# Three chained layers on one core: copies moved between engines, half of the split jobs moved to a later stage, a memset between record scatters

## The chip, the cores and the metric

One NeuronCore of a Trainium2 chip runs one program. The metric is the device time of one execution in microseconds (us), the median of three runs. The engines are named PE (TensorE matmul, with PEld for its weight loads), DVE (VectorE), ACT (ScalarE), POOL (GpSimd) and SP (SyncE, which here does little but issue DMAs). A `q` behind a name is that engine's queue of instructions or transfers.

## The reference

The output of each function is the input of the next:

```
def attn(x, h):                      # x (4, 5696, 128), h (5696, 128)
    L = 2 * S
    y = irfft(rfft(x, n=L, axis=1) * rfft(h, n=L, axis=0), n=L, axis=1)[:, :S]

def moe(x, phi, w1, w2):             # x (22784, 128), phi (128, 32): 8 experts, 4 slots each
    logits = x @ phi
    d = softmax(logits, axis=0);  slot_input = d.T @ x
    slot_out[e] = relu(slot_input[e] @ w1[e]) @ w2[e]
    return softmax(logits, axis=1) @ slot_out

def moe2(x, modality_id, w_gate, modality_bias, w1, w2):   # 8 experts, 128 -> 1024 -> 128
    logits = x @ w_gate + modality_bias[modality_id]
    e_idx = argmax(logits); gate_w = softmax(logits)[e_idx]
    out[t] = gate_w[t] * (relu(x[t] @ w1[e]) @ w2[e]),  e = e_idx[t]
```

## The kernel before, in words

**Convolution** (`conv_spectra`, to about 337 us of the span). The long convolution is a product of spectra, and the transforms are matrix products with constant tables. The sequences h and then four batches of x pass one after the other: 16 blocks `psa` (L122) whose result four copies in `columns` spread into A, two on ACT (L127) and two on DVE (L133), and then products `psx` (L188), multiplications on DVE and POOL, and transposes. `load` fetches the next sequence over SP's queue. Beside this runs a side task, the **split jobs** (`w2split_jobs`): the 32 pieces of `moe2_w2` are fetched (`wa`, 128 KB each, L312), cast on ACT (L317), subtracted on DVE (L318) and stored as a high and a low part into `s_wsc` (L320). Seven jobs run in the blocks of each batch of x, one more at i = 18, the rest at the end.

**Slot logits** (`slot_logits`). 32 tiles `psi` (L400), three buffers of PSUM, copied out by ACT (L403) and DVE (L405) by turns. SP loads for this and the next step in this order: two big `yl` (L373), four `Bt` (L381), four ring buffers (L352), then eight `c_iv` (L381). Then `psb` (L421) and the maxima.

**Slot inputs** (`slot_inputs`). `less` (L534) subtracts the maximum, three small pieces on DVE and seven large ones on POOL, and ACT takes the exponential (L538). `columns` makes 16 blocks `psw` with the same four copies; where its `swap` holds, the second copy of the first half goes to DVE (L131) in place of ACT. Then 23 rounds of `px` (L568), a copy on DVE (L569) and `psS` (L575), with the ring of loads beside them; the slot experts follow, whose weights are loaded last.

**Routing and routed experts.** The gate picks an expert for each token, and positions `posi` in a list sorted by expert. `scatter` (L1036) writes 178 columns of 128 records (136 bytes each) into `s_rec` with indirect DMAs on POOL, one instruction for each column. Up to 90 tiles of 256 tokens then run: `load_rec`, `ph` (L1126), ReLU on ACT and a subtraction on DVE (L1128, L1129), `acc` (L1139 to L1141), a transpose, and two indirect scatters into the output on POOL (`store`, L1164). A tile can't start before the first columns are scattered that can hold its records: tile 0 needs 18, tiles 5 to 8 need 34, 14 to 23 need 64, 24 to 39 need 96, 40 to 55 need 128, and from tile 56 on all 178. The order on POOL is written out beforehand by `share`: 64 records, 3 output scatters, 78 records, then records and output scatters in turn, and at the end only output scatters; with the last record 46 output scatters (23 tiles) stand ahead of it. `YBUF = 31` buffers hold finished tiles that wait for their scatter.

```
n = NG - len(pending)
late = max(0, len(outs) - 2 * YBUF + 6)
new = max(0, GB[chunk_of(k + 3) + 1] - n, min(ready[0] - n, m - late))
scatter(new)
store(max(late, m - new), k - 2)
```

Of the kernel before, what the change touches and what calls it, by code (L numbers as in the profile page):

```python
# [12 lines left out]
F32 = mybir.dt.float32  # L13
# [74 lines left out]
def dma89(eng, out, in_):  # L88
    eng.dma_start(out[0:80], in_[0:80])
    eng.dma_start(out[80:N1], in_[80:N1])  # L90
# [6 lines left out]
def keep_warm(nc, pp, t, n, **k):  # L97

    ps = pp.tile([128, 128], F32, name="warm", **k)
    for _ in range(n):  # L100
        nc.tensor.matmul(ps, t, t, start=True, stop=True)
# [14 lines left out]
def columns(nc, tc, pp, xs, fw1, put, swap=False, **k):  # L116


    ps = pp.tile([128, 4, 256], F32, **k)
    pv = ps[:, :, :4 * NPAIR].rearrange("p i (r k e) -> p r i k e", r=2, e=2)  # L120
    for i, x in enumerate(xs):
        nc.tensor.matmul(ps[:, i, :4 * NPAIR], x, fw1, start=True, stop=True)  # L122
    for j in range(2):
        for r in range(2):
            o, v = put(r, j), pv[64 * j:64 * j + 64, r]
            if j == 0 and not (swap and r):
                i = nc.scalar.copy(o, v)  # L127
                tc.declare_no_dep(i.ins, group="half1", reason="other lanes of PSUM, other columns of the result")
                tc.add_to_no_dep_group("half0", i.ins)
            elif j == 0:  # L130
                nc.vector.tensor_copy(o, v)  # L131
            else:
                i = nc.vector.tensor_copy(o, v)  # L133
                tc.declare_no_dep(i.ins, group="half0", reason="other lanes of PSUM, other columns of the result")
                tc.add_to_no_dep_group("half1", i.ins)


def conv_spectra(nc, tc, I, R, P, jobs, xr, ahead):

    G, ident, phi, fw1 = P["G"], P["ident"], P["phi"], P["fw1"]  # L140
    with tc.tile_pool(name="p1", bufs=1) as sp, tc.tile_pool(name="p1p", bufs=2, space=PS) as pp:
# [14 lines left out]
            else:  # L156
                nc.gpsimd.tensor_copy(o, v)  # L157

        def load(q, c):

            if q < len(seqs):
                kind, b = seqs[q]
                src = (I["x"][b] if kind == "x" else I["h"]).rearrange("(p s) d -> p s d", s=N2)
                dma89(nc.sync, xt[:, 16 * c:16 * c + 16], src[:, 16 * c:16 * c + 16])

        def st1(c):

# [2 lines left out]
                    lambda r, j: A[64 * r:64 * r + 64, :, 64 * j + d:64 * j + d + 4].rearrange("p k d e -> p d k e"),  # L170
                    name="psa", tag="psa", bufs=2)

        for c in range(4):
            load(0, c)
        keep_warm(nc, pp, P["ones"], NWARM, tag="psa", bufs=2)

        pl = pp.tile([128, 4, 128], F32, name="psl", tag="psl", bufs=1)
# [93 lines left out]
        for q in range(len(seqs)):  # L271
            z = Seq(q)
            if q == 0:
                for c in range(NXS):
                    spread(c)
            for c in range(16):
                st1(c)
                if c + NXS < 16:
                    spread(c + NXS)
                if q > 0 and jobs and c % 2 and c < 14:  # L280
                    jobs.pop(0)(sp)
                if q == 0 and c < 6:
                    P["loadG"](c)
            for i in range(NB):
                for _ in range(2 if i == 0 else 1):
                    if tail:
                        tail.pop(0)()
                z.step(i)
                if q > 0 and i == 18 and jobs:
                    jobs.pop(0)(sp)  # L290
                if i % 4 == 0 and i < 16:
                    load(q + 1, i // 4)
                if q + 1 < len(seqs) and i % 2 and i >= NB - 2 * NXS:
                    spread((i - NB) // 2 + NXS, nc.scalar)
                if q == B and i % 2 == 0 and 2 <= i < 18:
                    ahead(i // 2 - 1)
            tail = z.tail()
        for t in tail:
            t()
        while jobs:  # L300
            jobs.pop(0)(sp)
def w2split_jobs(nc, I, R):

    got = {}
    n = 4 * NE

    def job(k):
        def run(sp):
            if k < n:
                e, h = divmod(k, 4)  # L310
                a = got[k] = sp.tile([128, 2, 128], F32, name="wa", tag="wa", bufs=2)
                nc.sync.dma_start(a, I["moe2_w2"][e].rearrange("(c p) d -> p c d", p=128)[:, 2 * h:2 * h + 2])  # L312
            if k >= 1:
                e, h = divmod(k - 1, 4)
                a = got.pop(k - 1)
                w = sp.tile([128, 2, 2, 128], F32R, name="ws", tag="ws", bufs=2)
                nc.scalar.copy(w[:, 0], a)  # L317
                nc.vector.tensor_tensor(w[:, 1], a, w[:, 0].bitcast(F32), op=ALU.subtract)  # L318
                o = R["wsc"][e].rearrange("p (r f) -> p r f", r=2)[:, :, 256 * h:256 * h + 256]
                nc.sync.dma_start(o, w.rearrange("p r c d -> p r (c d)").bitcast(F32))  # L320
        return run
    return [job(k) for k in range(n + 1)]
# [35 lines left out]
        return s.rearrange("p (b k d) -> p b k d", b=B, k=YB)[:, b, k % YB, :]  # L358


def slot_logits(nc, tc, I, R, P, a2, xr, yr, Lf):

    ident, ones, iv1 = P["ident"], P["ones"], P["iv1"]
    L = Lf.rearrange("p (j s) -> p j s", s=N2)
# [2 lines left out]
    with tc.tile_pool(name="p2", bufs=1, reuse_waits="tile") as sp, tc.tile_pool(name="p2p", bufs=3, space=PS, reuse_waits="tile") as pp:  # L367
# [7 lines left out]
        def load_B(c):  # L375
            if c < NBT or c >= N2 // BC - NBT:
                t = sp.tile([128, BC, 2, N1], F32, name="Bt", tag="Bt", bufs=NBT)
            else:
                w = 2 * BC * N1
                t = xr[:, w * (c - NBT):w * (c - NBT) + w].rearrange("p (x r s) -> p x r s", x=BC, r=2)  # L380
            nc.sync.dma_start(t, I["c_iv2"][:, BC * c:BC * c + BC])  # L381
            Bt[c] = t
# [9 lines left out]
        pst = [pp.tile([128, 4, 128], F32, name=f"psi{i}", tag=f"a{i}", bufs=1) for i in range(3)]  # L392
        for t in pst:
            nc.vector.memset(t[64:], 0.0)
        for b in range(B):
            yl = yls[b].rearrange("p (k s) -> p k s", s=NS)
            for s in range(0, NS, 4):
                ps = pst[(b * NS + s) // 4 % 3]
                for j in range(4):
                    nc.tensor.matmul(ps[:N1, j], yl[:, :, s + j], iv1, start=True, stop=True)  # L400
                o = A2[:96, :, b * NS + s:b * NS + s + 4].rearrange("p x j -> p j x")
                if s % 8 == 0:
                    nc.scalar.copy(o, ps[:96])  # L403
                else:
                    nc.vector.tensor_copy(o, ps[:96])  # L405
            if b == 1:
                for c in range(NBT, N2 // BC - NBT):
                    load_B(c)
        SC = 8
        mx = sp.tile([N1, N2 // 4, NS], F32, name="mx")  # L410
        m1 = sp.tile([N1, NS], F32, name="m1")
# [101 lines left out]
def slot_inputs(nc, tc, I, R, P, a2, yr, L, cm, c, prefetch, cT):  # L513

    G, fw1 = P["G"], P["fw1"]
    with tc.tile_pool(name="p3p", bufs=2, space=PS, reuse_waits="tile") as pp:
# [8 lines left out]
        jobs = row_softmax_jobs(nc, R, c, scratch(NG))  # L525
        Ssb, den = scratch(128), scratch(NS)
        fill = token_bias(nc, I, scratch(2 * NG), scratch(2 * NE))
        assert used[0] <= 14 * F
        JC = 16

# [10 lines left out]
        less(0, 4, nc.vector)  # L541
        less(4, 8, nc.vector)
        less(8, JC, nc.vector)
        for j in range(JC, 128, JC):
            less(j, j + JC, nc.gpsimd)
        weights(0, 4)
# [1 line left out]
        weights(8, JC)  # L548
        for j in range(0, 128, 8):
            columns(nc, tc, pp, [L[:, j + i:j + i + 2].rearrange("p j s -> p (j s)") for i in (0, 2, 4, 6)], fw1,  # L550
                    lambda r, i: AW[64 * r:64 * r + 64, :, j + i:j + i + 7:2].rearrange("p k j e -> p j k e"), j % 24 == 8,
                    name="psw", tag="a", bufs=2)
            if j + JC < 128:
                weights(j + JC, j + JC + 8)
            if j % JC == JC - 8:
                yr.load()
# [7 lines left out]
        def X(i):  # L564
            n = nk4(i)
            ps = pp.tile([128, 4, 128], F32, name="px3", tag="x", bufs=2)
            for m in range(n):
                nc.tensor.matmul(ps[:, m], G[:, 4 * i + m, :], AW[:, 2 * i + m // 2, :, m % 2], start=True, stop=True)  # L568
            nc.vector.tensor_copy(fw[i % 2][:, :n], ps[:, :n])  # L569

        def dot(i):
            for m in range(nk4(i)):
# [435 lines left out]
def routed_experts(nc, tc, R, P, out, ro, tabs):  # L1008

    ident, rec, posi = P["ident"], ro.rec, ro.posi  # L1010
    with tc.tile_pool(name="p6", bufs=1, reuse_waits="tile") as sp, tc.tile_pool(name="p6p", bufs=1, space=PS, reuse_waits="tile") as pp:
# [20 lines left out]
        def scatter(n):  # L1032
            for _ in range(n):
                c, g = pending.pop(0)
                need(0, g + 1)
                i = nc.gpsimd.indirect_dma_start(R["rec"], bass.IndirectOffsetOnAxis(ap=posi[:, g:g + 1], axis=0), rec[:, g, :], None,  # L1036
                                                 bounds_check=SPARE * TM - 1, oob_is_err=False)
                for q in range(NC):
                    tc.declare_no_dep(i.ins, group=f"rec{q}", reason="positions of tokens are distinct")
                tc.declare_no_dep(i.ins, group="recl", reason="a tile is loaded after its last token was scattered")  # L1040
                tc.declare_no_dep(i.ins, group="pad", reason="rows after the last token")
                tc.add_to_no_dep_group(f"rec{c}", i.ins)
# [203 lines left out]
def build(nc, tc, I, O, dbg=None):  # L1246
# [14 lines left out]
    with tc.tile_pool(name="const", bufs=1) as cp:  # L1261
# [35 lines left out]
            n = min(N1, k + 23)  # L1297
            nc.sync.dma_start(x[:, k:n], R["ylt"][b, :, k:n])
        with tc.manual_schedule():
            conv_spectra(nc, tc, I, R, P, w2split_jobs(nc, I, R), xr,  # L1300
                         ahead)

        pac, pa = pool("pa")
# [19 lines left out]
            for h in range(4):  # L1323
                nc.sync.dma_start(mw[:, 2 * h:2 * h + 2], I["moe2_w1"][2 * h:2 * h + 2].rearrange("e p f -> p e f"))
        with tc.manual_schedule():
            cm = slot_logits(nc, tc, I, R, P, a2, xr, yr, Lf)
        cqc, cq = pool("cq", side="right")
        c = cq.tile([128, NG, NS], F32, name="c")
        g2 = G.rearrange("p k x -> p (k x)")
# [143 lines left out]
```

## Time and profile before

| | |
|---|---|
| median of 3 runs | 1235.42 us (1233.53 to 1237.55) |
| the profiled execution, its own time | 1235.99 us |
| its span, first to last instruction | 1234.2 us |
| busy: PE, DVE, ACT, POOL | 931.4, 651.2, 594.4, 581.0 us |
| instructions | 23513 |
| mean granted TensorE clock | 0.878 |

Busy time counts an engine's instructions that compute or, on POOL, prepare a DMA. The page's slices cut the span into 40 equal parts of 30.9 us; a digit is the busy share in tenths. The chain is followed back from the last instruction, at each step to what released it. "Another core or an unknown queue" is a stretch for which the trace shows no releaser, and "issue" one in which the engine waited for nothing that the profile shows.

### The profile page before, as it was taken

The page shows a single profiled execution, that of the slowest core. Times are in us where ns is not written, and L with a number is a line of the kernel's source. Part 1 is how long each engine was busy: PE and PEld are TensorE (multiplying, and loading weights), DVE is VectorE, ACT ScalarE, POOL GpSimd, SP SyncE. Part 2 cuts the span into 40 slices and gives each one's busy share as a digit, 9 for nine tenths or more (in the row PEclk, how much of TensorE's full clock was granted, in tenths as well). Part 3 has the DMA queues.
Part 4 walks back from the last instruction along what each step waited for, and adds up shares of the span by engine and source line. Part 5 has one row for each costly group of instructions (what it writes and reads, how often), then busy time and mean ns, then how long its engine had stood idle before and what let it go on. Part 6 is the DMA issues. An engine that isn't in the chain of part 4 may idle for free.

```text
span 1234.2 us, 23513 instructions
## 1 busy us (share of the span) xinstructions
PE 931.4 (75%) x7670; PEld 845.8 (69%) x7670; DVE 651.2 (53%) x1225; ACT 594.4 (48%) x1338; POOL 581.0 (47%) x677
## 2 busy tenths in 40 slices
PE   7989999999999789933189231810119999999996
PEld 7988888888799777613189231810119999999996
DVE  2577767777637885432068121600016666666663
ACT  2574747565544542210068021600017777777774
POOL 2127566565830433157701755277554444444443
PEclk8999999999999999966589665965559999999999
DMA  9437585766783889833110000011001111111112
GB/s 290 106 92 221 155 233 177 217 193 188 251 313 106 292 288 399 262 88 114 27 47 11 15 13 12 13 30 32 28 29 42 38 38 40 37 40 38 40 39 77
DMA packets 101901, 144.20 MB, mean 117 GB/s; under 512 B 26044, under 2 KB 80764, under 8 KB 99228
## 3 DMA queue, kind: packets, MB, share of 16 engines
q1 hardware_dynamic: 90056, 126.82, 32.9%
q0 software_dynamic: 11456, 14.79, 4.0%
q8 instruction: 64, 1.05, 0.4%
q10 hardware_dynamic: 264, 1.05, 0.2%
q14 instruction: 61, 0.50, 0.1%
HBM read 220.23 MB, written 57.77 MB: 225 GB/s over the span
## 4 chain that ended last, share of the span: by engine, by line
PE 62%; another core or an unknown queue 17%; DVE 9%; issue 5%; ACT 4%; DMA 2%; POOL 0%; SPq 0%; ACTq 0%; POOLq 0%; DVEq 0%
PE psx L188 9%; PE ph L1126 8%; PE acc L1141 7%; PE acc L1140 7%; PE acc L1139 7%; PE psa L122 6%; PE psi L400 3%; PE psy L94 3%; PE pso L94 3%; DVE A L133 3%; PE psl L226 2%; PE psb L421 2%; PE psS L575 1%; PE px L568 1%
## 5 line engine op out<-in xcount | busy, mean ns | idle before, releaser
L1129 DVE SCALAR_TENSOR_TENSOR hl<-ph,hh 128x512 fp32r<-128x512 f32 x360 | 247.9, 691 | 256.4 <-issue 134.5
L1164 POOL DMA_INDIRECT out<-y,rt x180 | 174.9, 972 | 218.4 <-ACT y L1153 173.6
L1128 ACT ACTIVATE hh<-ph 128x512 fp32r<-128x512 f32 x360 | 216.2, 602 | 107.3 <-PE ph L1126 41.0
L1126 PE MATMUL ph<-x,wm 128*128 128x256 f32 x720 | 164.6, 312 | 103.8 <-issue 65.2
L1036 POOL DMA_INDIRECT s_rec<-rec,posi x178 | 173.4, 974 | 134.9 <-issue 52.9
L1140 PE MATMUL acc<-hl,wo 128*128 128x256 f32 x720 | 208.5, 290 | 3.7 <-issue 3.7
L1141 PE MATMUL acc<-hh,wo 128*128 128x256 f32 x720 | 208.3, 289 | 3.5 <-issue 3.5
L1139 PE MATMUL acc<-hh,wo 128*128 128x256 f32 x720 | 209.0, 290 | 0.3 <-issue 0.3
L1126 PEld LDWEIGHTS ph<-x,wm 128*128 128x128 f32 x720 | 115.0, 199 | 107.4 <-issue 66.4
L1141 PEld LDWEIGHTS acc<-hh,wo 128*128 128x128 f32 x720 | 142.9, 198 | 3.8 <-issue 3.8
L1140 PEld LDWEIGHTS acc<-hl,wo 128*128 128x128 f32 x720 | 143.1, 199 | 2.7 <-issue 2.5
L1139 PEld LDWEIGHTS acc<-hh,wo 128*128 128x128 f32 x720 | 142.9, 198 | 0.0
L188 PE MATMUL psx<-G,A 128*128 128x128 f32 x890 | 124.5, 287 | 2.5 <-DVE A L133 1.3
L188 PEld LDWEIGHTS psx<-G,A 128*128 128x128 f32 x890 | 111.9, 196 | 19.8 <-DVE Y L199 13.2
L122 PE MATMUL psa<-fw,xs 128*128 128x180 f32 x640 | 111.0, 328 | 13.0 <-POOL xs L157 6.8
L122 PEld LDWEIGHTS psa<-fw,xs 128*128 128x128 f32 x640 | 100.7, 200 | 23.5 <-POOL xs L157 14.4
L133 DVE COPY A<-psa 64x360 f32<-64x360 f32 x160 | 88.2, 551 | 37.3 <-PE psa L122 33.5
L127 ACT COPY A<-psa 64x360 f32<-64x360 f32 x160 | 83.6, 522 | 42.2 <-PE psa L122 39.0
L201 POOL TENSOR_TENSOR Y<-Y,V 128x256 f32<-128x256 f32 (+1 forms) x92 | 65.4, 711 | 63.8 <-DVE V L200 57.8
L94 PE MATMUL pso<-ident,yT 128*128 128x128 f32 x180 | 39.9, 305 | 71.1 <-ACT yT L1145 50.6
L212 ACT COPY yt<-psy 128x512 f32<-128x512 f32 (+1 forms) x92 | 52.6, 572 | 79.4 <-PE psy L94 50.2
L157 POOL COPY xs<-xr 89x512 f32<-89x512 f32 x68 | 45.7, 673 | 94.6 <-PE psa L122 74.1
(200 smaller groups left out, 1414.2 us busy)
## 6 DMA issues: line engine op xcount, KB each, us to landing
wo<-s_wsc SPq DMA_DIRECT2D x90, 1024.0 KB
wm<-s_mwsc SPq DMA_DIRECT2D x180, 256.0 KB
s_yt<-yt SPq DMA_DIRECT2D x88, 256.0 KB
xr<-x SPq DMA_DIRECT2D x16, 640.0 KB
xr<-s_yt SPq DMA_DIRECT2D x18, 512.0 KB
s_wsc<-ws SPq DMA_DIRECT2D x32, 256.0 KB
L<-s_yt SPq DMA_DIRECT2D x16, 512.0 KB
s_ylt<-ylt SPq DMA_DIRECT2D x20, 256.0 KB
```

The source lines that it names most:

```text
L94: nc.tensor.transpose(out, in_, ident)
L122: nc.tensor.matmul(ps[:, i, :4 * NPAIR], x, fw1, start=True, stop=True)
L133: i = nc.vector.tensor_copy(o, v)
L188: nc.tensor.matmul(ps[:, m, :], A[:, 2 * i + m // 2, :, m % 2], G[:, 4 * i + m, :], start=True, stop=True)
L1036: i = nc.gpsimd.indirect_dma_start(R["rec"], bass.IndirectOffsetOnAxis(ap=posi[:, g:g + 1], axis=0), rec[:, g, :], None, bounds_check=SPAR ...
L1126: nc.tensor.matmul(ps[:, TM * j:TM * j + TM], wm[k % 3][:, 128 * f:128 * f + 128], x[k], start=True, stop=True)
L1128: nc.scalar.activation(o, ps, AF.Relu)
L1129: nc.vector.scalar_tensor_tensor(hl[:, 2 * q:2 * q + 2].rearrange("p j t -> p (j t)"), ps, 0.0, o.bitcast(F32), op0=ALU.max, op1=ALU.subtract)
L1139: nc.tensor.matmul(acc[k], wh, hh[:, f], start=(f == 0), stop=False)
L1140: nc.tensor.matmul(acc[k], wh, hl[:, f], start=False, stop=False)
L1141: nc.tensor.matmul(acc[k], wl, hh[:, f], start=False, stop=(f == 7))
L1164: i = nc.gpsimd.indirect_dma_start(out, bass.IndirectOffsetOnAxis(ap=r[:, j, NS + 1:RW].bitcast(I32), axis=0), y[:, j, :], None, bounds_ch ...
```

## The change

- h is loaded half over SP's and half over ACT's queue.
- `columns` makes its four copies in the order ACT, DVE, DVE, and last the one that `swap` gives to DVE or leaves to ACT; `swap` holds for 8 of the 16 `psw` blocks, not 5.
- In the convolution the split jobs run at every fourth block, and 16 of 32 are left for `psi`, where one runs at every second tile, with its buffers in the free end of Lf.
- A one-column copy on POOL (`pause`) waits for the last of DVE's three `less` pieces before POOL starts its own.
- The copies of `px` go to ACT for i < 13.
- A memset of 128x64 on POOL stands ahead of each of the 178 record scatters.

```diff
-    for j in range(2):
-        for r in range(2):
+    for j, r in ((0, 0), (1, 0), (1, 1), (0, 1)):
...
+            load(0, c + 2, nc.scalar)
...
-                if q > 0 and jobs and c % 2 and c < 14:
+                if q > 0 and c % 4 == 3 and c < 14:
                     jobs.pop(0)(sp)
...
-        while jobs:
-            jobs.pop(0)(sp)
+        jobs[0](sp, load=False)
...
+        free = 2 * YLW
+        def split(name, k):
+            if name == "wa":
+                return Lf[:, free + 256 * (k % 3):free + 256 * (k % 3) + 256].rearrange("p (c d) -> p c d", c=2)
+            w = Lf[:, free + 768 + 512 * (k % 3):free + 768 + 512 * (k % 3) + 512]
+            return w.rearrange("p (r c d) -> p r c d", r=2, c=2).bitcast(F32R)
...
                     nc.vector.tensor_copy(o, ps[:96])
+                if jobs and s % 8 == 0:
+                    jobs.pop(0)(split)
...
+        nc.gpsimd.tensor_copy(pause, L[:N1, JC - 1, :1])
         for j in range(JC, 128, JC):
             less(j, j + JC, nc.gpsimd)
...
-                    lambda r, i: AW[64 * r:64 * r + 64, :, j + i:j + i + 7:2].rearrange("p k j e -> p j k e"), j % 24 == 8,
+                    lambda r, i: AW[64 * r:64 * r + 64, :, j + i:j + i + 7:2].rearrange("p k j e -> p j k e"), j % 16 == 8,
...
-            nc.vector.tensor_copy(fw[i % 2][:, :n], ps[:, :n])
+            if i < 13:
+                nc.scalar.copy(fw[i % 2][:, :n], ps[:, :n])
+            else:
+                nc.vector.tensor_copy(fw[i % 2][:, :n], ps[:, :n])
...
                 need(0, g + 1)
+                nc.gpsimd.memset(P["iv1"][:, :64], 0.0)
                 i = nc.gpsimd.indirect_dma_start(R["rec"], bass.IndirectOffsetOnAxis(ap=posi[:, g:g + 1], axis=0), rec[:, g, :], None,
```

POOL at the start of the routing, before (the routed lists begin with the identity's cast, L1371; `s_rec<-rec,posi` is a record scatter, `out<-y,rt` an output scatter):

```order
L1371 CAST identr<-ident 128x128
L1036 DMA s_rec<-rec,posi 184576x34 x18
L806 IOTA rec 128x42
L1036 DMA s_rec<-rec,posi 184576x34 x46
L1164 DMA out<-y,rt 22784x128 x3
L1036 DMA s_rec<-rec,posi 184576x34 x78
```

The same place of POOL after the change (`iv_77` is iv1, no longer read by then):

```order
L1389 CAST identr<-ident 128x128
L1052 MEMSET iv_77 128x64
L1053 DMA s_rec<-rec,posi 184576x34
L1052 MEMSET iv_77 128x64
L1053 DMA s_rec<-rec,posi 184576x34
```

A memset stands ahead of each scatter, so no two record scatters stand next to each other; the output scatters have none.

SP at the loads for `psi` after the change (L372 and L380 are L373 and L381 of before, L351 is L352; `L<-moe_w` is a load of `wa`, `s_wsc<-L` a store of a split):

```order
L372 DMA L<-s_ylt 128x2848 x2
L380 DMA Bt<-c_iv 128x712 x4
L351 DMA xr<-s_yt 128x1024 x2
L351 DMA ring<-s_yt 128x1024 x2
L311 DMA L<-moe_w 128x2x128 x2
L319 DMA s_wsc<-L 256x1x256
L311 DMA L<-moe_w 128x2x128
```

DVE in the first tiles of `psi` after the change; ACT has a cast (L316) in the same way after each of its copies but the first:

```order
L393 MEMSET psi_3456 64x512
L412 COPY A_3425<-psi_3455 96x4x128
L317 TENSOR_TENSOR L<-L 128x256
L412 COPY A_3425<-psi_3454 96x4x128
L317 TENSOR_TENSOR L<-L 128x256
L412 COPY A_3425<-psi_3456 96x4x128
```

In the list of before the copies stand one after the other; now a step of a split job, which waits for a load that SP issues behind ten others, stands between the first and the second copy of DVE. The eight `c_iv` loads that followed the ring loads now stand behind seven of these stores.

## Rows read from the trace of the kernel before

**Rows 1.** The page: busy tenths in 40 slices, and the chain by engine.

```profile
PE   7989999999999789933189231810119999999996
POOL 2127566565830433157701755277554444444443
...
PE 62%; another core or an unknown queue 17%; DVE 9%; issue 5%; ACT 4%; DMA 2%; POOL 0%; SPq 0%; ACTq 0%; POOLq 0%; DVEq 0%
```

**Rows 2.** The chain, 530 to 930 us, two long pieces: start, us, what.

```profile
533.42 19.59 another core or an unknown queue
...
576.30 44.74 another core or an unknown queue
```

**Rows 3.** Stretches: from:to, us, busy us (instructions) by engine, clock, DMA share, GB/s.

```profile
core 0: us, PE busy (x) PEld busy (x) DVE busy (x) ACT busy (x) POOL busy (x), PEclk, DMA share, GB/s
583.00:621.00 38.00, 5.58 (x16) 4.03 (x15) 0.00 (x0) 0.00 (x0) 24.29 (x25) 0.50 0.13 29
799.00:863.00 64.00, 7.17 (x36) 6.58 (x36) 2.37 (x4) 3.36 (x8) 48.63 (x51) 0.58 0.11 31
863.00:883.00 20.00, 0.70 (x3) 0.70 (x4) 0.98 (x2) 1.17 (x3) 9.73 (x11) 0.50 0.07 23
920.00:1226.00 306.00, 298.64 (x2395) 285.49 (x2394) 202.46 (x331) 232.58 (x599) 131.39 (x136) 0.99 0.15 43
```

**Rows 4.** POOL in order of time: start, us, line, idle before and its releaser.

```profile
528.69 0.97 POOL L1036 DMA_INDIRECT s_rec<-rec,posi  x1 [0.30 <-issue]
529.97 0.97 POOL L1036 DMA_INDIRECT s_rec<-rec,posi  x1 [0.30 <-issue]
...
555.28 0.21 POOL L806 IOTA rec<- 128x42 int32 x1 [5.19 <-DVE xr L730]
556.07 1.14 POOL L1036 DMA_INDIRECT s_rec<-rec,posi  x1 [0.58 <-issue]
557.52 0.97 POOL L1036 DMA_INDIRECT s_rec<-rec,posi  x1 [0.30 <-issue]
```

**Rows 5.** Line 1036 alone: count, shortest/median/longest ns, first and last start.

```profile
L1036 POOL DMA_INDIRECT s_rec<-rec,posi x178: 969/972/1169, 527.2 to 919.4; - x178
```

**Rows 6.** PE inside and behind the record burst of 556 to 615 us.

```profile
589.49 0.37 PE L101 MATMUL warm<-ones 128*128 128x128 f32 x1 [2.45 <-issue]
...
623.90 2.07 PE L1126 MATMUL ph<-x,wm 128*128 128x256 f32 x8 [0.46 <-ACT x L1117]
```

**Rows 7.** A memset of nearly this size on POOL.

```profile
504.90 0.16 POOL L1367 MEMSET pad<- 128x68 f32 x1 [27.46 <-PE e L637]
```

**Rows 8.** SP's DMA issues for psi, in order of time.

```profile
338.78 2.34 SPq L373 DMA_DIRECT2D L<-s_ylt  x2
...
350.37 10.38 SPq L381 DMA_DIRECT2D xr<-c_iv  x8
```

**Rows 9.** The same loads: count, KB each.

```profile
xr<-c_iv SPq DMA_DIRECT2D x8, 356.0 KB
```

**Rows 10.** Stretches of psi and px, columns as in the third group.

```profile
337.00:378.00 41.00, 40.93 (x257) 40.63 (x257) 16.54 (x18) 16.89 (x18) 13.03 (x4) 0.96 0.63 241
356.00:364.00 8.00, 8.00 (x53) 8.00 (x53) 3.59 (x4) 3.08 (x3) 0.00 (x0) 1.00 1.03 400
364.00:380.00 16.00, 14.63 (x96) 14.47 (x95) 6.42 (x7) 6.16 (x6) 0.00 (x0) 1.00 0.03 10
446.00:502.00 56.00, 52.53 (x937) 44.24 (x935) 35.60 (x68) 13.22 (x22) 22.95 (x21) 1.00 0.99 353
```

**Rows 11.** Waits of 412 to 446 us (psw): total us, times, longest.

```profile
DVE A L131 <- ACT A L127: 5.7, 5, 1.6
...
ACT L L538 <- DVE L L534: 5.5, 3, 2.1
```

**Rows 12.** Waits of 446 to 502 us (px, psS).

```profile
PEld psS L575 <- DVE A L569: 4.7, 7, 0.8
```

**Rows 13.** The chain of 495 to 525 us, its longest piece.

```profile
507.00 9.07 DMA A<-moe_w
```

**Rows 14.** Waits of 134 to 157 us (the psa blocks of one batch).

```profile
PE psa L122 <- DVE A L133: 1.2, 3, 0.4
```

**Rows 15.** Busy tenths of the DMA engines, 0 to 20 us.

```profile
DMA  0003955999998999999999999999899998699899
```

More of the change, by code (lines that the diff above doesn't have):

```diff
@@ L122, in columns @@
         nc.tensor.matmul(ps[:, i, :4 * NPAIR], x, fw1, start=True, stop=True)
-    for j in range(2):
-        for r in range(2):
[L125 to L135, printed above, removed]
+    for j, r in ((0, 0), (1, 0), (1, 1), (0, 1)):
+        o, v = put(r, j), pv[64 * j:64 * j + 64, r]
+        if j == 0 and not (swap and r):
+            i = nc.scalar.copy(o, v)
+            tc.declare_no_dep(i.ins, group="half1", reason="other lanes of PSUM, other columns of the result")
+            tc.add_to_no_dep_group("half0", i.ins)
+        elif j == 0:
+            nc.vector.tensor_copy(o, v)
+        else:
+            i = nc.vector.tensor_copy(o, v)
+            tc.declare_no_dep(i.ins, group="half0", reason="other lanes of PSUM, other columns of the result")
+            tc.add_to_no_dep_group("half1", i.ins)
 def conv_spectra(nc, tc, I, R, P, jobs, xr, ahead):
@@ L157, in spread, with load @@
                 nc.gpsimd.tensor_copy(o, v)
-        def load(q, c):
+        def load(q, c, eng=nc.sync):
             if q < len(seqs):
@@ L163, in load @@
                 src = (I["x"][b] if kind == "x" else I["h"]).rearrange("(p s) d -> p s d", s=N2)
-                dma89(nc.sync, xt[:, 16 * c:16 * c + 16], src[:, 16 * c:16 * c + 16])
+                dma89(eng, xt[:, 16 * c:16 * c + 16], src[:, 16 * c:16 * c + 16])
         def st1(c):
@@ L171, in st1 @@
                     name="psa", tag="psa", bufs=2)
-        for c in range(4):
+        for c in range(2):
             load(0, c)
+            load(0, c + 2, nc.scalar)
         keep_warm(nc, pp, P["ones"], NWARM, tag="psa", bufs=2)
@@ L307, in job, with run @@
     def job(k):
-        def run(sp):
-            if k < n:
+        def run(sp, load=True):
+            if load and k < n:
                 e, h = divmod(k, 4)
-                a = got[k] = sp.tile([128, 2, 128], F32, name="wa", tag="wa", bufs=2)
+                a = got[k] = sp("wa", k) if callable(sp) else sp.tile([128, 2, 128], F32, name="wa", tag="wa", bufs=2)
                 nc.sync.dma_start(a, I["moe2_w2"][e].rearrange("(c p) d -> p c d", p=128)[:, 2 * h:2 * h + 2])
-            if k >= 1:
+            if k - 1 in got:
                 e, h = divmod(k - 1, 4)
                 a = got.pop(k - 1)
-                w = sp.tile([128, 2, 2, 128], F32R, name="ws", tag="ws", bufs=2)
+                w = sp("ws", k) if callable(sp) else sp.tile([128, 2, 2, 128], F32R, name="ws", tag="ws", bufs=2)
                 nc.scalar.copy(w[:, 0], a)
@@ L358, in get, with slot_logits @@
         return s.rearrange("p (b k d) -> p b k d", b=B, k=YB)[:, b, k % YB, :]
-def slot_logits(nc, tc, I, R, P, a2, xr, yr, Lf):
+def slot_logits(nc, tc, I, R, P, a2, xr, yr, Lf, jobs):
     ident, ones, iv1 = P["ident"], P["ones"], P["iv1"]
@@ L408, in slot_logits @@
                     load_B(c)
+        while jobs:
+            jobs.pop(0)(split)
         SC = 8
@@ L527, in slot_inputs @@
         fill = token_bias(nc, I, scratch(2 * NG), scratch(2 * NE))
+        pause = scratch(1)[:N1]
         assert used[0] <= 14 * F
@@ L568, in X @@
                 nc.tensor.matmul(ps[:, m], G[:, 4 * i + m, :], AW[:, 2 * i + m // 2, :, m % 2], start=True, stop=True)
-            nc.vector.tensor_copy(fw[i % 2][:, :n], ps[:, :n])
+            if i < 13:
+                nc.scalar.copy(fw[i % 2][:, :n], ps[:, :n])
+            else:
+                nc.vector.tensor_copy(fw[i % 2][:, :n], ps[:, :n])
         def dot(i):
@@ L1299, in build @@
         with tc.manual_schedule():
-            conv_spectra(nc, tc, I, R, P, w2split_jobs(nc, I, R), xr,
+            jobs = w2split_jobs(nc, I, R)
+            conv_spectra(nc, tc, I, R, P, jobs, xr,
                          ahead)
@@ L1325, in build @@
         with tc.manual_schedule():
-            cm = slot_logits(nc, tc, I, R, P, a2, xr, yr, Lf)
+            cm = slot_logits(nc, tc, I, R, P, a2, xr, yr, Lf, jobs)
         cqc, cq = pool("cq", side="right")
```

## The prediction, made before the result was known

> **What bounds the kernel now.** I began with the page's slices. The reader is to see a hole there: PE stands at 7 to 9 tenths up to the 17th slice and at 9 again from the 31st on, and between them, from about 525 to 925 us, at 3 or less in ten of 13 slices, while POOL stands at 5 to 7 in nine of them [rows 1]. The chain gives 17% of the span to "another core or an unknown queue" and 5% to "issue" [rows 1]. On one core there is no other core, so these are waits with no releaser that the trace knows; the longest piece takes 44.74 us from 576.30 on [rows 2]. Next I cut that region into stretches. From 583 to 621 us PE ran 16 instructions, DVE and ACT none, at a granted clock of 0.50 (the 1.2 GHz level), DMA 13% busy, POOL the only engine at work. From 799 to 863 PE was busy 7.17 of 64 us. In the last stretch, where only output scatters are left, PE is busy 298.64 of 306 us [rows 3].
>
> So what does POOL do in the hole? It runs record scatters back to back: each 0.97 us, 0.30 us apart, so 1.28 us from start to start [rows 4], 178 of them between 527.2 and 919.4 us [rows 5]. Meanwhile the other engines wait for nothing in the program: the warming matmuls of PE, which need only a constant, come one in 0.37 + 2.45 = 2.82 us, "issue" in front of each [rows 6]. I read this as a shared resource that the other engines need for each instruction and that scatters at 1.28 us fill. At which spacing it clears is bounded by two stretches. At 2.25 us (136 scatters in 306 us) nothing is missing. At 1.8 us (11 in 20 us, 863 to 883) PE is still at 0.70 of 20 us, but these come behind 51 scatters in 64 us, whose arrears may still have been worked off [rows 3]. The limit is between 1.28 and 2.25, and 1.8 is not proof either way. The first two fifths of the span, by contrast, are bound by PE, with DVE and ACT close.
>
> **The change part by part. The memset** carries the forecast. 178 are added, all on POOL, and nothing else on POOL moves but one copy. A memset of 128x68 took 0.16 us [rows 7]; this one has 128x64, so at least 0.16 is added and the spacing s is at least 1.28 + 0.16 = 1.44. What a scatter costs behind another kind of instruction is shown once: behind the IOTA 0.58 us of idle time, then 1.45 us until the next one starts [rows 4], so s is at most 0.16 + 0.58 + 1.45 = 2.19. I take 1.65: the scatter's own surcharge there (1.45 for 1.28, +0.17) and the memset, but not the idle time, since that IOTA came inside the hole, where every engine is late.
>
> If scatters at 1.65 us leave the others free, POOL sets the end of the records and PE runs beside it. The first scatter comes at 527 + 4 (the 4 is the sum of the other parts, below) = 531. Then 178 x 1.65 = 294, 46 output scatters ahead of the last record at 1.28 = 59, and about 10 for POOL's waits for positions and finished tiles (chosen): the last record at 894. PE's first tile loses the wait of 44.74 us: 623.9 - 44.7 + 4 = 583 [rows 2, 6]. At 306 us for 68 tiles, 4.5 us each [rows 3], 54 tiles would be done by 826, before the records are. They can't go further: from tile 56 on all 178 columns are needed, and 23 stored tiles + 31 buffers = 54. So 36 tiles remain at 894: 162 us, and 10 us from the end of the last stretch (1226) to the run's own 1236: 1066.
>
> One thing is late next. With the last record 54 - 23 = 31 tiles wait for their scatters, 62 of them, which POOL then issues back to back and without memsets: 62 x 1.28 = 79 us. Output scatters mixed with records did starve PE (7.17 of 64 us is 0.11 [rows 3]); output scatters alone at 1.28 us aren't shown. Between no loss and 0.89 x 79 = 70 us I take half, 35. That gives 1101.
>
> **psi.** PE needs 41 us for 32 tiles, 1.28 each, and idles nowhere [rows 10]. Now ACT and DVE have a split step between copies, and the first needs a load that SP issues behind the two yl, four Bt and four ring loads, which fill the DMA engines from 338.78 on [rows 8]. When will it land? In the run before, everything including the eight c_iv behind it was in by about 364 (DMA share 1.03 until then, 0.03 after [rows 10]); the c_iv are 8 x 356 KB = 2.85 MB [rows 9], 7.1 us at 400 GB/s, so the earlier ones end at 357. The split load then lands at about 358. With a cast, a subtraction and the copy behind it PE's seventh tile, due at 337.2 + 6 x 1.28 = 345, gets its buffer at about 360: +13 us, allowing for the bounds 0 (the transfers interleave) and +17. The c_iv loads now stand behind seven split stores, and the next split load behind them: again 7.1 us of transfers, of which three buffers hide about half: +3 (0 to 4). Together +16. In the run before DMA was free from 364 on, so nothing later needs these loads sooner.
>
> **psw.** DVE waits 5.7 us for ACT in the swapped blocks, which the new order takes away; I take -5 (-1.5 to -5.7). ACT waits 5.5 us for DVE's three pieces of less, which run beside POOL's [rows 11]; the pause leaves DVE alone first: -2 (0 to -3), since PE's first block is then next.
>
> **px.** PE's weight loads wait 4.7 us for DVE's copies [rows 12], so moving 13 copies to an idle ACT could give up to -5. But the DMA share is 0.99 from 446 to 502 [rows 10], and the slot experts then wait 9.07 us for weights [rows 13]. An earlier px mostly lengthens that wait: -1 (0 to -5).
>
> **The convolution.** In 23 us of psa PE waits 1.2 us for DVE's copies [rows 14], which a split step had delayed: four batches, -4 (0 to -9 with the weight loads). The copies' order changes nothing there, as each engine keeps its own two.
>
> **h.** The DMA engines are full from 2 us on [rows 15], so a second queue has nothing to add: 0 (-2 to +2). The Trainium skill (DMA: Bandwidth & Descriptors, Issuing engines are not separate DMA queues) says that issuing from several engines at once saves only the issuing sequencer's time; by it the sum would be less by a part of the 3 us over which SP issues these loads. The trace agrees with it in the full slices.
>
> Sum of these: +16 - 7 - 1 - 4 = +4, between -15 and +20. The sum is made against the profiled execution, 1235.99 us, 0.6 above the median of the three runs; a spread of 4 us in those runs means that about 0.3% is what can be told from no change.
>
> **The rivals.** *No relief*: s = 1.65 is still too dense, or the starved engines lack something that the spacing doesn't touch. Then the record bursts, which are on the chain, only get longer: 178 x (1.65 - 1.28) = 66, and with the +4 about 1306 (1268 at s = 1.44). For it speaks the stretch at 1.8 us; against it, that the hole opens and closes with the bursts and not with the work of any other engine. It decides if the needed spacing is above the one that the memset makes. The Trainium skill (Runtime: NRT & Kernel Launch, Instruction fetch mechanics) says that feeding instructions to an engine is mostly hidden; by that rule starved sequencers at 2.82 us an instruction should not be, and a gap between scatters would give them nothing. The matmul rows contradict its first half; no row here decides the second.
>
> *Half relief*: record bursts are free, but the mixed part or the output scatters starve PE throughout; with s at its upper bound the last record comes at 990 and the end at 990 + 172 + 70 = 1232.
>
> *The memset hides*: it runs in the 0.30 us "issue" gap, s stays near 1.28, and the change doesn't space the scatters. Then 1236 + 4 = 1240, the psi stall deciding the sign.
>
> *psi doesn't stall*, a side case: everything 13 us earlier, 1088.
>
> **How the numbers follow.** Relief 0.70, half relief 0.08, no relief 0.17, hidden 0.05. The first two are faster but for a sliver at 1232; the hidden case is about equally same or slower. Faster by over 0.3% 0.76, within 0.3% 0.03, slower 0.21. Predicted 1101. With relief alone s from 1.44 to 2.19 and the store arrears from 0 to 70 give 1030 to 1232; the range adds the hidden case at 1240 and leaves the no-relief one out: 1030 to 1245.
>
> **What would show it.** The record scatters' start-to-start distance (1.65), PE near 9 tenths from about 583 us on, "unknown queue" gone from the chain, PE waiting for records before tile 54, the last record near 894, back-to-back output scatters behind it and whether PE sags there; in psi one PE gap of some 13 us near 345; in psw no wait of L130 for ACT. It is wrong if scatters at the new distance still leave PE with an instruction every 2.8 us, or if the distance is near 2.2.

## The result: slower by 1.2%, and the profile after

The changed kernel takes 1253.93 us (median of 4 runs, 1249.79 to 1255.5) against 1236.49 (4 runs) of the kernel before: ratio 1.0124, with a 95% interval of 1.0099 to 1.0149. Here and below the ratio is not the quotient of the two medians (1.0141 here), but close to it. The forecast was 1101 in a range up to 1245, with 0.21 for slower.

The page after, PE and POOL in 40 slices of 31.3 us, and the chain by engine:

```profile
PE   7989999999956989954149352810109999999996
POOL 2138475665810047067740768186764444444443
...
PE 61%; another core or an unknown queue 16%; DMA 6%; ACT 6%; issue 5%; DVE 4%; ACTq 1%; POOL 0%; SPq 0%; POOLq 0%; DVEq 0%
```

Beside [rows 1] two things are to be seen. The hole of POOL's record bursts is still there, and the chain still gives 16% to an unknown releaser. And PE has a new dent at the 12th and 13th slice, while DMA's share of the chain has grown from 2% to 6%. The dent is psi. PE there, in order of time (the list ends at 400 us, so that its last line lacks seven matmuls):

```profile
335.93 8.63 PE L407 MATMUL psi<-iv,xr 128*89 128x128 f32 x48
359.19 13.90 PE L407 MATMUL psi<-iv,xr 128*89 128x128 f32 x80 [14.63 <-DVE A L412]
372.92 7.60 PE L407 MATMUL psi<-iv,L 128*89 128x128 f32 x48
387.84 12.45 PE L407 MATMUL psi<-iv,L 128*89 128x128 f32 x73 [7.32 <-DVE A L412]
```

After six tiles (48 matmuls) PE waits 14.63 us, later 7.32. ACT shows for what, a line for each cast that came late:

```profile
357.34 0.41 ACT L316 CAST L<-L 128x256 fp32r<-128x256 f32 x1 [15.44 <-DMA L<-moe_w]
...
386.00 0.41 ACT L316 CAST L<-L 128x256 fp32r<-128x256 f32 x1 [8.13 <-DMA L<-moe_w]
```

And POOL, where the forecast stood, in order of time:

```profile
547.80 0.97 POOL L1053 DMA_INDIRECT s_rec<-rec,posi  x1 [0.17 <-issue]
548.76 0.17 POOL L1052 MEMSET iv<- 128x64 f32 x1
549.10 0.97 POOL L1053 DMA_INDIRECT s_rec<-rec,posi  x1 [0.16 <-issue]
550.07 0.17 POOL L1052 MEMSET iv<- 128x64 f32 x1
550.39 0.98 POOL L1053 DMA_INDIRECT s_rec<-rec,posi  x1 [0.16 <-issue]
```

The memset takes 0.17 us and stands inside what was a gap of 0.30 [rows 4]: scatters come 1.30 us apart (the median), not 1.28. Two stretches, columns as in [rows 3]:

```profile
583.00:639.00 56.00, 9.32 (x30) 7.02 (x29) 1.72 (x6) 0.30 (x1) 45.11 (x80) 0.53 0.23 57
937.00:1244.00 307.00, 298.07 (x2394) 285.13 (x2394) 202.19 (x330) 232.12 (x597) 130.10 (x134) 0.99 0.15 43
```

In the burst PE still runs only 30 matmuls in 56 us (16 in 38 before), at a clock of 0.53, and the last stretch is nearly as long as before. First starts by stage, from the traces:

| first start, us | before | after | after minus before | e3 (below) |
|---|---|---|---|---|
| psi | 337.2 | 335.9 | -1.3 | 337.3 |
| psb | 379.5 | 404.1 | +24.6 | 379.5 |
| less | 412.7 | 438.9 | +26.2 | 412.7 |
| px | 446.3 | 469.1 | +22.8 | 442.8 |
| slot experts | 502.9 | 522.0 | +19.1 | 495.7 |
| first record scatter | 527.2 | 546.3 | +19.1 | 519.4 |
| first tile (ph) | 623.9 | 642.1 | +18.2 | 615.1 |
| last record scatter | 919.4 | 935.2 | +15.8 | 910.0 |
| end of the span | 1234.2 | 1253.7 | +19.5 | 1227.5 |

The loss arises between the first psi and the first psb: 42.3 us became 68.2, 25.9 more. What comes behind wins some of it back, and the stretch from the last record scatter to the end is 3.7 us longer than before.

### The profile page after: what moved, and what is told of

It reads as the page before. It is cut to its first block, busy times and chain, and to the rows that moved or that the text cites. A ratio compares the mean times of both kernels' runs of the same rounds, so it can differ in the third digit from the quotient of the medians.

```text
span 1253.7 us, 23727 instructions
## 1 busy us (share of the span) xinstructions
PE 935.5 (75%) x7670; PEld 850.6 (68%) x7670; DVE 645.7 (52%) x1215; ACT 598.9 (48%) x1348; POOL 609.6 (49%) x856
## 4 chain that ended last, share of the span: by engine, by line
PE 61%; another core or an unknown queue 16%; DMA 6%; ACT 6%; issue 5%; DVE 4%; ACTq 1%; POOL 0%; SPq 0%; POOLq 0%; DVEq 0%
PE ph L1143 9%; PE psx L188 9%; PE psa L122 6%; PE acc L1158 6%; PE acc L1157 6%; PE acc L1156 6%; PE psy L94 3%; PE pso L94 3%; PE psl L226 2%; DMA s_mwsc<-G 2%; PE psb L432 2%; PE px L581 2%; ACT yT L1162 2%; PE psS L591 2%
## 5 line engine op out<-in xcount | busy, mean ns | idle before, releaser
L212 ACT COPY yt<-psy 128x512 f32<-128x512 f32 (+1 forms) x92 | 52.6, 572 | 77.7 <-PE psy L94 52.5
```

## The experiments

Ratios are to the kernel before on the same chip, with 95% intervals, from three rounds each.

**Without the memsets** (e1).

```diff
-                nc.gpsimd.memset(P["iv1"][:, :64], 0.0)
```

> The changed kernel without the 178 memsets. Theory (the memset runs inside the 0.30 us gap between scatters and changes nothing; the loss is psi's): 1250 to 1258 us, the record scatters 1.28 us apart again in place of 1.295, the time lost in psi unchanged. Rival (the memsets themselves cost time, since they lengthen the bursts and delay every scatter): about 1236 to 1245.

1255.98 us, 1.0147 (1.0124 to 1.0170). The loss isn't the memsets'; they are worth nothing that the intervals tell apart here.

**The memset alone** (e2): the kernel before with that one line.

> The kernel before with the memset as its only edit. Theory (hidden): 1233 to 1240, spacing 1.295, psi at its old 41 us. Rival (the memset costs): about 1245 to 1255. The forecast's own idea (relief) would give about 1100.

1233.31 us, 0.9972 (0.9959 to 0.9985): hidden, as the theory has it, with a gain of some 3 us.

**All split jobs back in the convolution** (e3).

```diff
-                if q > 0 and c % 4 == 3 and c < 14:
+                if q > 0 and jobs and c % 2 and c < 14:
...
-        jobs[0](sp, load=False)
+        while jobs:
+            jobs.pop(0)(sp)
```

> The changed kernel with all split jobs back in the convolution, where they were. Theory (psi's two stalls and what follows them cost 26 us, the convolution gains about 1 from fewer jobs): 1226 to 1231, below both kernels. Rival (the psi stall only uncovers time that a later stage limited by DMA would have taken anyway): 1240 to 1254.

1225.83 us, 0.9908 (0.9886 to 0.9930): 28 us below the changed kernel, and faster than before. Nothing of the psi stall would have been lost further on anyway. The table's last column shows what the rest of the change is worth: less to px takes 30.1 in place of 33.6 us, px to the slot experts 52.9 in place of 56.6.

**Four memsets of 128x128 ahead of each record scatter**, on the kernel before (e4).

```diff
+                for _ in range(4):
+                    nc.gpsimd.memset(P["iv1"], 0.0)
```

> The kernel before with four memsets of 128x128 ahead of each record scatter: about 0.975 + 4 x 0.2 + 0.16 = 1.94 us from scatter to scatter, so that POOL truly spaces them. Theory of the forecast (a scatter every 1.28 us fills something that the others need; spacing frees them): 1080 to 1180, PE near 9 tenths from about 583 us on. Rival (the spacing frees nothing, the bursts only get longer): 1300 to 1350.

1296.23 us, 1.0483 (1.0461 to 1.0505). The time fits neither sentence (it lies just under the rival's range): the distance became 2.53 us, not 1.94, and both mechanisms are seen at once. Stretches of this run:

```profile
580.00:620.00 40.00, 22.34 (x139) 21.66 (x139) 15.66 (x30) 16.29 (x42) 28.78 (x80) 0.75 0.14 39
740.00:780.00 40.00, 3.46 (x17) 3.50 (x18) 2.44 (x5) 3.16 (x8) 28.48 (x79) 0.50 0.05 10
1040.00:1100.00 60.00, 10.85 (x60) 9.79 (x59) 4.04 (x7) 5.17 (x13) 42.13 (x44) 0.59 0.14 49
```

Tile 0 starts at 575.7, not 623.9, so four memsets between scatters do free the other engines. But the last record comes at 1035.8, and tiles wait for theirs (from 740 to 780 us PE idles for that reason, not for want of instructions). Behind the last record 44 output scatters in 60 us starve PE again.

**Two memsets, and three** (e5, e8): as e4 with `range(2)` and `range(3)`.

> The kernel before with two memsets of 128x128 ahead of each record scatter. One memset left the distance at 1.295 us and four made it 2.53, so two should give 1.5 to 1.9. Theory A (the others are freed as soon as a scatter comes less often than about every 1.43 us): PE near 9 tenths through the bursts, last record near 880 to 910, time 1080 to 1150. Theory B (they are free only well above 2 us): starved as before, bursts longer, 1250 to 1310.

> The kernel before with three memsets of 128x128 ahead of each record scatter: 2.0 to 2.2 us from scatter to scatter. Theory A: as with two memsets but the records end 60 to 90 us later, 1150 to 1220. Theory B: 1270 to 1310, most of the bursts still starved.

Two: 1204.86 us, 0.9733 (0.9701 to 0.9765), scatters about 2.0 us apart, tile 0 at 569.7, last record at 943.4. Three: 1252.43 us, 1.0125 (1.0091 to 1.0159), 2.26 apart, tile 0 at 572.6, last record at 991.2. Theory A holds in what limits the run: PE is free in the bursts, and each 0.26 us more delays the last record by some 45 to 48 us. Its times were too early, the upper ends of its ranges by 55 us (two) and 32 us (three), and for three it forecast a gain where a loss was measured.

**Two memsets ahead of output scatters too** (e6): the same loop in `store`.

> As the run with two memsets, and two ahead of each output scatter as well. If output scatters back to back starve PE in the same way as records: the stretch behind the last record, which starved PE with four memsets (busy 10.85 of 60 us), is gone, and the end is set by POOL, 358 scatters at 1.5 to 1.9 us from 527 on plus its waits: 1120 to 1220. If they don't, only slower than the run without them by up to 60 us.

1275.08 us, 1.0297 (1.0259 to 1.0335). PE's last `ph` begins at 1132.1, 56 us earlier than in e5, so output scatters back to back do starve PE; but POOL goes on to 1266.5. POOL is the end now, later than expected.

**Two memsets of 128x8** (e9), on the kernel before.

```diff
+                for _ in range(2):
+                    nc.gpsimd.memset(P["iv1"][:, :8], 0.0)
```

> The kernel before with two memsets of 128x8 (0.04 us each) ahead of each record scatter. With two of 128x128 the distance was 2.03 us: 0.97 for the scatter, 0.49 for the memsets and 0.55 of idle time behind them, where one memset had left only 0.16. If that idle time comes with the second memset and not with its length, the distance is about 1.6 and the records end about 75 us earlier than with the long ones: 1120 to 1190, if 1.6 still frees PE. If 1.6 does not free it: 1240 to 1290. If the idle time goes with the length, the distance stays near 1.3 and the time near 1233.

1187.50 us, 0.9587 (0.9567 to 0.9606). The time lies in the first range, but partly by luck, since the distance is not the one that the range was made for. POOL in order of time, and three stretches of this run:

```profile
561.71 0.98 POOL L1038 DMA_INDIRECT s_rec<-rec,posi  x1 [0.70 <-issue]
562.67 0.29 POOL L1037 MEMSET iv<- 128x8 f32 x2
563.61 0.98 POOL L1038 DMA_INDIRECT s_rec<-rec,posi  x1 [0.64 <-issue]
```

```profile
580.00:620.00 40.00, 35.51 (x281) 34.91 (x279) 28.82 (x58) 28.61 (x73) 25.09 (x62) 0.91 0.13 37
940.00:990.00 50.00, 7.79 (x36) 7.13 (x36) 2.37 (x4) 2.73 (x6) 34.31 (x36) 0.53 0.15 49
1040.00:1180.00 140.00, 133.01 (x1075) 126.80 (x1073) 89.17 (x146) 103.34 (x266) 60.66 (x63) 1.00 0.16 49
```

1.90 us apart (1.6 was expected), tile 0 at 570.4, last record at 925.9. PE is busy 35.51 of 40 us inside the burst where it had 5.58 of 38 [rows 3], and behind the last record it starves beside 36 scatters in 50 us. SP's record loads wait 52.6 us for scatters from 580 to 930.

**The same ahead of output scatters too** (e10).

> The same two small memsets ahead of output scatters too. With two long ones there POOL itself set the end (358 scatters at 2.03 us). At 1.6 us they take 573 us from 527 on, 1100, plus waits: 1115 to 1170, and the starved stretch behind the last record is gone. If 1.6 does not free PE: 1270 to 1330.

1238.92 us, 1.0001 (0.9989 to 1.0012). PE's last `ph` begins at 1110.6, 61 us before e9's, but from 1120 on PE does nothing and POOL scatters on to 1230. The time lies some 70 us above the expected range, because the distance is 1.90 for records and 1.97 for output scatters and not 1.6.

**psi's split loads on ACT's queue** (e7), on the changed kernel.

```diff
-                nc.sync.dma_start(a, I["moe2_w2"][e]...
+                (nc.scalar if callable(sp) else nc.sync).dma_start(a, I["moe2_w2"][e]...
```

> The changed kernel with the split loads of psi issued on ACT's queue and not behind the ten and then the eight big loads on SP's. Theory (the two stalls of 14.6 and 7.3 us are a place in a queue, not bandwidth): both shrink to under 3 us and the run takes 1228 to 1237. Rival (the DMA engines are full at that time, so that any queue waits as long): 1248 to 1256.

1250.99 us, 1.0096 (1.0058 to 1.0133): the rival's time, but only in part its reason. ACT's waits from 336 to 404 us in this run, total, times, longest:

```profile
ACT L L316 <- DMA L<-moe_w: 13.7, 6, 7.2
ACT L L316 <- DMA s_wsc<-L: 13.2, 2, 9.8
```

In the changed kernel the first of these was 25.0 us, longest 15.4, and the second not there. The first load was issued at 338.83 and its cast began at 350.32, so a queue of its own saves some 7 us and no more while the DMA engines are full (busy share 0.98 from 339 to 350 us); and the stores of the split parts, still on SP's queue behind the ring loads, then hold ACT's buffers. PE's first stall shrinks to 6.43 us and one of 8.94 follows.

**The split jobs in psi's last 16 tiles** (e11), on the changed kernel.

```diff
-                if jobs and s % 8 == 0:
+                if jobs and b >= 2:
```

> The changed kernel with the 16 split jobs of psi at each of its last 16 tiles and not at every second tile: their loads and stores then come behind the eight c_iv loads, which in the kernel before were in by 364 us of the span, when the 22nd tile begins. Theory (the split loads wait because the DMA engines are full from 341 to 364 us, whatever their queue): one stall of up to 8 us in place of 14.6 and 7.3, and 1232 to 1242. Rival (the steps on ACT and DVE between the copies are themselves too much for psi): 1248 to 1256.

1247.89 us, 1.0078 (1.0054 to 1.0101): 6 us above the theory's range and at the edge of the rival's. ACT in this run, in order of time:

```profile
366.09 0.40 ACT L316 CAST L<-L 128x256 fp32r<-128x256 f32 x1 [6.99 <-DMA L<-moe_w]
...
370.53 0.40 ACT L316 CAST L<-L 128x256 fp32r<-128x256 f32 x1 [2.91 <-DMA L<-moe_w]
...
374.88 0.41 ACT L316 CAST L<-L 128x256 fp32r<-128x256 f32 x1 [2.37 <-DMA L<-moe_w]
...
379.74 0.40 ACT L316 CAST L<-L 128x256 fp32r<-128x256 f32 x1 [2.70 <-DMA L<-moe_w]
```

The long stall goes, but every second cast waits 2 to 3 us: SP issues a load only behind a store that waits for DVE, so with jobs at every tile the load's round trip is on the chain. ACT idles before these casts, so the rival's reason, too much work between the copies, is not what the trace shows. psi still takes 54.8 us (40.6 before) and psb waits 5 us behind it.

**What worked, together** (e12): e3 with two memsets of 128x8 ahead of each record scatter and ahead of every second output scatter (`if j == 0`).

> The changed kernel with all split jobs back in the convolution, two memsets of 128x8 in place of the one of 128x64 ahead of each record scatter, and two ahead of every second output scatter. If the gains add (10 us of the first, 51 of the second) without the third: about 1177. If pacing half of the output scatters also removes the starved stretch of some 75 us behind the last record without making POOL the end (134 scatters at 1.6 us from about 940 on): 1145 to 1165. If POOL becomes the end all the same: 1180 to 1200.

1166.06 us, 0.9458 (0.9425 to 0.9490), faster than both kernels and 1 us above the middle range. Two stretches:

```profile
930.00:1060.00 130.00, 124.26 (x1027) 122.32 (x1026) 85.10 (x145) 101.23 (x263) 86.66 (x160) 0.99 0.17 49
1110.00:1164.00 54.00, 0.00 (x0) 0.00 (x0) 0.00 (x0) 0.00 (x0) 32.03 (x58) 0.50 0.10 34
```

Behind the last record (933.2) PE is busy now. But PE is done at 1093.4, and the last 70 us are POOL's alone, so POOL has become the end as in the last case. The ratios of e3 and e9 multiplied give 0.950 against 0.9458 here, so the memsets ahead of output scatters are worth some 5 us, about as much as the intervals leave open; they were not run by themselves.

## Why the prediction was wrong

**The step that failed** is "at least 0.16 is added and the spacing s is at least 1.28 + 0.16 = 1.44". The 0.30 us of "issue" between two scatters was counted as part of each scatter's time; a short memset runs inside it. s was 1.30, and everything built on 1.65 or on the relief that it was to bring (the records at 894, tile 0 at 583, 1066, 1101) fell with it. This was the rival "the memset hides", which got 0.05 and 1240; the memset is in fact worth between nothing and 3 us (e1 against the changed kernel, e2). The lower bound was thus no bound: the row for the gap was there [rows 4], and "in the gap" should have been its lower end and its own large case.

**The mechanism behind it was right** for wider distances, and no row of before could show it: at 1.90 us and above the other engines are free during the bursts, tile 0 comes at 570 to 576 (579 without the upstream +4), PE runs, and the records limit the tiles. In e9 54.75 tiles have passed `ph` when the last record scatter starts (54 were forecast; 24.25 in the kernel before). With s = 1.90 the forecast's own sum, without the 4, puts the last record at 527 + 338 + 59 + 10 = 934 (e9: 925.9), and 934 + 162 + 10 + 70 = 1176 with the full store arrears (e9: 1187.5). "One thing is late next" is what the runs show, at its upper end. The rival "no relief" is refuted for 1.90 and above; it is what the changed kernel does at 1.30. At the forecast's own 1.65 nothing was run. The Trainium skill (Runtime: NRT & Kernel Launch, Instruction fetch mechanics) calls the cost of fetching the next block of instructions mostly hidden, and the prediction read it as saying that a gap would give nothing; e9 says that it gives much. The prediction took the slow matmuls to contradict the page. They do not, since they do not wait for a block of code each: the code loads among the DMA queues of the kernel before, 583 to 621 us (packets, MB, share of 16 engines), are one, while PE ran 16 matmuls:

```profile
q8 instruction: 1, 0.02, 0.2%
```

**psi** was right in mechanism and too small in size. The split load was expected at about 358 us, and its cast began at 357.34; the first stall was +13 against 14.63 (the forecast's own instants, 345 and 360, give 15). The second was +3 against 7.32: the c_iv loads were issued from 374.19 to 379, the load behind them landed at 386, and of these 11.8 us, not 7.1, the three buffers hide less than half. With the short waits at the end, from the first psi to the first psb +25.9 against +16. e3 shows that it reaches the end in full; e7 and e11 that neither a queue nor a later place alone takes it away, since a full set of DMA engines, the stores in SP's order and the round trip each bind in turn.

**psw** with the pause: -7 against -3.4. The pause gave what it should (the three pieces of less take 1.36 us, not 4.77), but in psw PE still waits on ACT's exponentials. **px**: -1 against -3.7. The argument that full DMA engines would take the gain back was wrong: the stretch to the slot experts got shorter, and the slot experts no longer than before. **The convolution**: -4 against -1.3. **h**: within 0.3 of nothing.

The sum of these was forecast at +4 and measured at +19 (the slot experts' row of the table): 10 of the 15 are psi, 4 are gains that were put too high, less the one put too low, and the rest arises between psb and less, for which there was no term.

Two readings were slightly off and move nothing: POOL stands at 5 to 7 in all ten slices of [rows 1] where PE is at 3 or less, not in nine, and 44 output scatters stand ahead of the last record in the trace, not 46.

## What to carry to other kernels

An idle gap between two instructions of one engine is not part of their price: what is put there may cost nothing and, if it was meant as a pause, do nothing. Before a side task is moved under a stage that waits for nothing, look at what the DMA queues carry in that stretch, and in what order: an in-order engine that waits for a small load behind some 6 MB of others stops the copies behind it too. If one engine's bursts starve all others, spacing them can pay well, but the engine's own total then becomes the next bound, so only as much spacing as frees the others. In e12's last 70 us nobody else works, and leaving the memsets out there is the next thing to try; it was not run.

## What the runs showed of the hardware

While indirect scatters run back to back on POOL, PE's warming matmuls, which wait for nothing in the program, come one in some 2.8 us [rows 6], and DVE and ACT run nothing for 38 us [rows 3], ACT because it waits for PE. At a distance of 1.30 us this is little better, at 1.90, 2.0, 2.26 and 2.53 us PE is free. No run lies between 1.30 and 1.90. Which resource is short stays open: in that stretch the DMA engines are 13% busy [rows 3] and one block of code is loaded, so neither of these is full.

Whether the distance frees the others, or the second instruction between two scatters, is not separated, since every run that frees them has at least two memsets; one long memset was not tried. One place speaks against the distance alone. In the changed kernel some scatters come 2.1 us apart, with one memset each, and PE still gets only one matmul per scatter. POOL first, then PE:

```profile
605.12 0.98 POOL L1053 DMA_INDIRECT s_rec<-rec,posi  x1 [0.60 <-issue]
607.27 0.98 POOL L1053 DMA_INDIRECT s_rec<-rec,posi  x1 [0.59 <-issue]
```

```profile
605.04 0.37 PE L101 MATMUL warm<-ones 128*128 128x128 f32 x1 [1.73 <-issue]
607.20 0.37 PE L101 MATMUL warm<-ones 128*128 128x128 f32 x1 [1.79 <-issue]
```

What makes the distance is odd too: one memset of 128x64 adds 0.02 us, two of 128x8 (0.29 together) add 0.62, most of it idle time (0.64 to 0.70) ahead of the next scatter. The jump comes with the second memset more than with its length: two of 128x128 give about 2.0. From there on each further one of 128x128 adds 0.26. The Trainium skill (Perfetto Trace Analysis, GPSIMD Engine Instruction) says to time POOL by the distance from start to start and not by the spans; the trace agrees, since no sum of spans here gives 1.30 or 1.90.
